# SyncE reads the register values of four expert tiles at once, for all tiles, in a fused attention and mixture-of-experts kernel

## The chip, the cores and the metric

One core of one Trainium2 chip runs the whole program. The metric is device time in microseconds of one execution, given as the median of several. The profile is of one execution; its times count from the span's start.

## What is computed

Attention over four images with keys that are pooled 4 x 4, then a mixture of eight experts in which each row goes to the one expert with the highest score:

```python
kv_pool = kv.reshape(B, H // r, r, W // r, r, C).mean(axis=(2, 4))
k = v = kv_pool.reshape(B, -1, C) @ w_sr
a = softmax(scale * (q @ k.transpose(0, 2, 1)))
x = (a @ v).reshape(B * S, D)                 # 49152 rows of 128
expert_idx = argmax(logits of x against expert_emb, axis=1)
for e in range(E):                            # 8 experts, F = 1024
    mask = expert_idx == e
    h = np.maximum(x[mask] @ w1[e], 0.0)
    out[mask] = gate_w[mask, None] * (h @ w2[e])
```

## The kernel before, in words

**Attention.** 96 steps of 512 query rows (`NSTEP`, `Q`). A step computes scores on TensorE (L810; the first 16 steps L803), takes the maximum on DVE (L821), the exponential on ACT (L840), and splits the result into two fp16 parts, `phi` and `plo`. SyncE issues two DMA transposes for each half of a step, `pthi` and `ptlo` (L904), and TensorE multiplies them with the values (L926). Queries come through a load (L702) and, in most steps, a DMA transpose `qT` (L790). Four steps are a group: its 2048 rows are scored against the experts, and POOL scatters them with indirect DMAs into the table `xs_rows`, each to the region of its expert (L207).

**Experts.** When a group is placed, `select` cuts from what lies in the regions eight tiles (`PER`) of 256 rows, each of one expert. It writes the first row of each tile into eight columns of `off_i` (L1454) and the row of the tile's weights in `w_prep` into eight columns of `wi_i` (L1373), with one instruction each, `wi_i` last. A value of `E * P` or more in `wi_i` means that the weights lie in the buffer already, and the copy is skipped. There are 184 such tiles (`NA`), and after them up to 23 of 128 rows for what is left over, in stages.

SyncE loads a tile. `load_w(t)` (L1563) takes the tile's value of `wi_i` into a register and issues a copy of 1026 KB of weights under a condition (L1568) into one of three buffers `wbuf`. `load(t)` (L1574) takes the value of `off_i`, issues a DMA transpose of 256 rows into `x` (L1592) and a small copy of gates and row numbers `m` (L1593). Both take the register from `value` (L1552), which has two ways: for the tiles up to `NA - PER` = 176 one register is read for one tile, with a check of its bounds (L1554); for the eight tiles after that and the remainder, the first tile of four reads four registers in one instruction without that check (L1557), and `held` keeps them for the other three. TensorE then computes the first layer (L1625), ACT and DVE the ReLU in two fp16 parts `hh` and `hl` (L1632, L1637), TensorE the second layer (L1661), ACT or DVE the gated output (L1681, L1684), and POOL scatters it into the output (L207).

**The order.** No order is left to the hardware: a planner in the program (`Plan.run`) simulates all engines while the kernel is built and writes the instructions in the order that it finds. `pl.add(engine, length, key, ...)` enters an operation with its planned length in us, a due time as key, and what it depends on. The planner takes the engine that is free first, and from its operations that are ready the one with the smallest key. For SyncE it also keeps a time `moved` at which the DMA engines will have moved what is queued, and adds a part for longer issues:

```python
turned = op.dur > 0.5
free[eng] = max(
    free[eng] + (0.55 if turned else 0.0), self.moved - (0.93 if turned else X["ahead"])
)
```

`X["ahead"]` is 2.284. `kw`, the key of a weight copy, is 1 us ahead of that of the tile's `x`, and `x` is due `X["lead"]` = 18.786 us ahead of the tile's first matmul. So a planned length of a SyncE operation sets when the planner holds the following transposes and loads for ready, and through them in which order it writes the work of the other engines.

Of the kernel before, what the change touches and what calls it, by code (L numbers as in the profile page):

```python
# [46 lines left out]
    lead=18.786, x=-14.465, r=0.691, s=-1.205, p=14.572, x0=3.032, r0=2.092, s0=1.377, p0=5.813, qt0=-0.263,  # L47
# [12 lines left out]
def attention_moe(  # L60
# [11 lines left out]
    nc = tc.nc  # L72
# [12 lines left out]
    Q = 512  # L85
# [8 lines left out]
    PER = G * Q // T  # L94
    NSEL = NGRP - LAG
    NA = NSEL * PER
    NTILE = NA + (NT - NA * T) // TR + E - 1
# [5 lines left out]
    OB = 8  # L103
    XB = 6
# [149 lines left out]
    class Plan:  # L254
# [9 lines left out]
        def add(self, eng, dur, key, fn, *deps, dma=None, take=None, free=None, hold=False, lands=False, port=False):  # L264
            op = Op(eng, dur, key, fn, deps, dma, take, free, hold, lands, port, self.stage)
            self.ops.append(op)
            return op
# [1279 lines left out]
    def size(t):  # L1547
        return T if t < NA else TR
# [1 line left out]
    held = {}  # L1550

    def value(name, src, t, top):  # L1552
        if t < NA - PER:
            return nc.sync.value_load(src[0:1, t : t + 1], min_val=0, max_val=top)  # L1554
        i = t // 4 * 4
        if (name, i) not in held:
            held[name, i] = nc.values_load_multi_w_load_instructions(  # L1557
                src[0:1, i : min(i + 4, NTILE)], engines=[nc.sync.engine], min_val=0, max_val=top,
                skip_runtime_bounds_check_because="the rows and weights of a tile are bounded where they are worked out",
            )[1]  # L1560
        return held[name, i][t - i]

    def load_w(t):  # L1563
        if NA <= t < NA + 2:
            wbuf.append(kvs.tile([P, WD], F16, tag="kvt", name=f"wbuf{WB + t - NA}", bufs=2))
        w = value("w", wi_i, t, E * P + 4096)
        row = nc.s_assert_within(w, 0, (E - 1) * P, skip_runtime_bounds_check_because="the copy is skipped then")
        nc.sync.dma_start(out=wbuf[turn_of(t)][:, :WC], in_=wprep[ds(row, P), :], cond=w < E * P)  # L1568

    xr, late = [], []  # L1570
    ML = 18
    XR = 4 * NK // (4 * TR)

    def load(t):  # L1574
        n = size(t)
        o = value("x", off_i, t, NROW - n)
        if t == NA - ML:
            late.append(wk.tile([P, NK], F32, tag="p", name="ml", bufs=NP))
        if t < NA:
            if t < NA - ML:  # L1580
                m = wk2.tile([P, n // P, 2], F32, tag="m", name=f"m{t}", bufs=OB + 2)
            else:
                m = late[0][:, (t - NA + ML) * 8 : (t - NA + ML) * 8 + n // P * 2].rearrange("p (j c) -> p j c", c=2)
            x = wk2.tile([P, 2, n], F16, tag="x", name=f"x_{t}", bufs=XB)
        else:
            i, j = divmod(t - NA, XR)
            if j == 0:
                xr.append(wk.tile([P, NK], F32, tag="p", name=f"xr{i}", bufs=NP).bitcast(F16))
            x = xr[i][:, j * 2 * n : (j + 1) * 2 * n].rearrange("p (h q) -> p h q", h=2)
            m = wk2.tile([P, n // P, 2], F32, tag="mr", name=f"m{t}", bufs=NTILE - NA)  # L1590
        src = xs[ds(o, n), :]
        a = nc.sync.dma_start(out=x, in_=src.bitcast(F16)[:, 0 : 2 * C], transpose=True)  # L1592
        b = nc.sync.dma_start(out=m, in_=src[:, CG : CG + 2].rearrange("(j p) c -> p j c", p=P))  # L1593
        if t < NA:
            for ins in (a, b):
                for key in keys[t // PER + LAG + 1 :]:
                    tc.declare_no_dep(ins.ins, group=key, reason="rows of earlier groups only")
                tc.add_to_no_dep_group("loads", ins.ins)
        ts[t].update(x=x, m=m)

    def turn_of(t):
        return t % WB if t < NA else (WB, WB + 1, *[(NA + i) % WB for i in range(WB)])[(t - NA) % (WB + 2)]
# [4 lines left out]
    def wide(t):  # L1607
        return t >= NA

    def units(t):  # L1610
        return NF * size(t) // 512
# [39 lines left out]
    def l2_lo(t, u):  # L1651
        l2_terms(t, u, ts[t].pop(("hl", u)), (0,))
# [53 lines left out]
    add, chain = pl.add, pl.chain  # L1706
    uses = {}

    def turn(tag, bufs):

        u = uses.setdefault(tag, [])
        return (u[-1][:1] if u else []) + (u[-bufs] if len(u) >= bufs else [])

    def took(tag, op):
        uses[tag].append([op])
        return op

    def reads(tag, *ops):
        uses[tag][-1].extend(ops)
# [121 lines left out]
    stores, v_whole, whole_k, kf_next = [], [], [], []  # L1841
# [295 lines left out]
    for k in range(NSTEP):  # L2137
        if k % SPB == SPB // 2 and k // SPB + 1 < B:
            kv_ops(k // SPB + 1)
        t = step_ops(k)  # L2140
        if k % G == G - 1:
            t = group_ops(k // G, t)
# [12 lines left out]
    def wb_turn(t):  # L2155
        u = uses.setdefault("wb", [])
        before = t - WB if t < NA else t - WB - 2
        return u[-1][:1] + u[before] if before >= 0 and not NA <= t < NA + 2 else []

    for t in range(NTILE):  # L2160
        pl.stage = sum(t >= NA + n for n in STAGES)
        s, n, nu = TM[t], t // PER, units(t)
        w = (X["di"] if KA + t * T // Q < NSTEP else X["db"]) / 8
        whole = t < NA
        deps = [x_open, chosen[n][-1], *placed[n + LAG]] if whole else [x_open, rest[-1], *x_pads, x_dummies, *placed[NGRP - 1]]
        tx, tm = ("mx", "m" if t < NA - ML else "ml") if whole else ("mxr", "mr")
        if t >= NA - ML:
            turn(tx, 1), turn(tm, 1)
        ld = add("SP", 2.5 if t < NA - PER else 1.5 if t % 4 else 2.5, s - (X["lead"] if whole else X["leadr"]), lambda t=t: load(t), *deps, *(turn(tx, XB) if whole else ()), *turn(tm, OB + 2 if t < NA - ML else NTILE), dma=1.3 * size(t) / Q)
        took(tx, ld)  # L2170
        took(tm, ld)
        first = NA <= t < NA + 2
        kw = TM[NA] - X["wr"] + 9.0 * (t - NA) if first else s - X["lead"] - 1.0 if whole else s - X["leadr"] - 8.0
        lw = took("wb", add(
            "SP", 0.5 if t < NA - PER else 0.2 if t % 4 else 1.2, kw, lambda t=t: load_w(t), *deps[:2], *stores, *wb_turn(t),
            dma=3.6 if t < WB or first or NA + 1 < t < NA + 7 else 0.08, hold=first,
        ))
        o1, o2, ol = None if whole else o1, None, None
        f = 512 / size(t)
        for u in range(nu):  # L2180
            key = s + (u + X["m"]) * w
            tag, swap = ("ph2", x_last) if wide(t) and u % 2 else ("ph", x_swap)
            own = None if tag == "ph2" else f"ph{t}_{u}"
            o1 = add(
                "PE", 0.65, key, lambda t=t, u=u: l1(t, u), ld, lw, swap, o1, *(() if own else turn(tag, 2)), take=own
            )
            if not own:
                took(tag, o1)
            k2 = key + X["l2"] * w
            hi = took("hh", add("ACT", 0.48, k2 - X["h"], lambda t=t, u=u: h_hi(t, u), o1, *turn("hh", 4)))  # L2190
            lo = took("hl", add("DVE", 0.6, k2 - X["h"] + 0.3, lambda t=t, u=u: h_lo(t, u), hi, *turn("hl", 6), free=own))
            if not own:
                reads(tag, hi, lo)
            po = "po2" if wide(t) and t % 2 else None
            took_po = None if po else f"po{t}"
            o2 = add(
                "PE", 0.45, k2, lambda t=t, u=u: l2(t, u), hi, o2, *((*turn(po, 1), x_last) if u == 0 and po else ()),
                take=took_po if u == 0 else None,
            )
            if u == 0 and po:  # L2200
                took(po, o2)
            reads("hh", o2, lo)
            ol = add("PE", 0.225, k2 + X["lb"] * w, lambda t=t, u=u: l2_lo(t, u), lo, o2, ol)
            reads("hl", ol)
        reads(tx, o1)
        if gated(t):
            g = add("DVE", 0.08, k2 - X["og"], lambda t=t: o_gate(t), ld, lw, port=True)
            reads("wb", g)
            o = took("o", add("ACT", 1.06 / f, k2 + 0.8, lambda t=t: o_out(t), g, ol, *turn("o", OB), free=took_po))
        else:  # L2210
            o = took("o", add("DVE", 0.66 / f, k2 + 0.8, lambda t=t: o_out(t), ol, *turn("o", OB), free=took_po))
        if po:
            reads(po, o)
        reads("wb", o)
        sc = [
            add("POOL", 1.12, k2 + 4.0 + 1.34 * j, lambda t=t, j=j: o_scatter(t, j), o, dma=0.2) for j in range(size(t) // P)
        ]
        reads("o", *sc)
        reads(tm, o, *sc)
# [38 lines left out]
```

## Time and profile before

| | us |
|---|---|
| median of 3 runs (1941.62 to 1948.85) | 1942.09 |
| the profiled execution's own time | 1946.91 |
| its span, first to last instruction | 1945.2 |
| TensorE matmuls busy in the span | 1906.0 |
| VectorE (DVE) busy | 1675.1 |
| ScalarE (ACT) busy | 1468.7 |
| GpSimd (POOL) busy | 1289.4 |

PE is TensorE's matmul row, PEld its row of weight loads. SP is SyncE; it computes nothing, and all that it does (register reads, waits, DMA issues) is shown in rows that are marked SPq and not counted as busy. A DMA issue's row lasts until SyncE has handed the DMA over; where the instruction waits for a semaphore, that may lie inside the row or ahead of it.

### The profile page before, as it was taken

What the parts mean: (1) busy time and instruction counts of PE and PEld (TensorE: products, weight loads), DVE (VectorE), ACT (ScalarE), POOL (GpSimd) and SP (SyncE); (2) the same over time, 40 slices, a digit from 0 to 9 for tenths busy, and PEclk for the clock granted to TensorE, in tenths of its full rate; (3) what the DMA queues carried; (4) which work ended last, traced back from release to release, by engine and by line L of the source; (5) the groups of instructions that cost most, each with busy time, mean ns of one, the idle gap of its engine ahead of it and who ended that gap; (6) DMA issues with size and microseconds to landing.
All of it is one profiled execution on the core that took longest, in us unless ns stands there. A gap on an engine that the chain in (4) does not pass through costs nothing. (4 is left out here: it accounts for less than half of the span.)

```text
span 1945.2 us, 63642 instructions
## 1 busy us (share of the span) xinstructions
PE 1906.0 (98%) x23536; PEld 1676.3 (86%) x23536; DVE 1675.1 (86%) x4037; ACT 1468.7 (76%) x3162; POOL 1289.4 (66%) x1857
## 2 busy tenths in 40 slices
PE   6999999999999999999999999999999999999998
PEld 5787788888888888888888888888888888889998
DVE  7899999988989879989989988998888888886655
ACT  4887877877787778877778877878878788775553
POOL 2547587678777777676676675756756766666654
PEclk9999999999999999999999999999999999999999
DMA  7998989889988999878989899887878677664353
GB/s 258 250 267 207 205 174 183 165 156 164 170 182 173 190 205 175 172 165 157 193 168 175 180 214 180 171 157 155 176 132 173 149 153 152 148 126 86 107 131 109
DMA packets 870922, 333.23 MB, mean 171 GB/s; under 512 B 825794, under 2 KB 836171, under 8 KB 868432
## 3 DMA queue, kind: packets, MB, share of 16 engines
q1 hardware_dynamic: 844624, 274.95, 71.4%
q0 software_dynamic: 24640, 53.53, 9.7%
q8 instruction: 186, 3.05, 0.7%
q14 instruction: 128, 1.05, 0.2%
q10 hardware_dynamic: 1344, 0.66, 0.1%
HBM read 271.41 MB, written 63.19 MB: 172 GB/s over the span
## 5 line engine op out<-in xcount | busy, mean ns | idle before, releaser
L1632 ACT ACTIVATE hh<-ph 128x512 f16<-128x512 f32 x754 | 447.6, 595 | 224.4 <-PE ph L1625 181.2
L1637 DVE SCALAR_TENSOR_TENSOR hl<-ph,hh 128x512 f16<-128x512 f32 x754 | 513.6, 684 | 109.6 <-ACT hh L1632 103.7
L1625 PE MATMUL ph<-x,wbuf 128*128 128x256 f16 x4416 | 593.2, 273 | 3.2 <-DMA wbuf<-w_prep 2.5
L207 POOL DMA_INDIRECT xs_rows<-rows,pi x384 | 442.0, 1151 | 176.5 <-issue 37.8
L207 POOL DMA_INDIRECT out_dram<-o,m x350 | 382.4, 1093 | 229.0 <-ACT o L1681 45.8
L1625 PEld LDWEIGHTS <-wbuf 128*128 128x128 f16 x4848 | 438.9, 98 | 67.4 <-DMA wbuf<-w_prep 2.9
L1661 PE MATMUL po<-wbuf,hh 128*128 128x128 f16 x6032 | 459.9, 219 | 2.9 <-DVE hl L1637 1.1
L1661 PEld LDWEIGHTS <-hh 128*128 128x128 f16 x6176 | 400.0, 98 | 20.6 <-issue 3.8
L810 PE MATMUL s<-k,qT 128*128 128x512 f16 (+1 forms) x1920 | 364.9, 326 | 1.4 <-DVE nm L821 1.4
L821 DVE CUSTOM_DVE_ANT_0 p<-s,scales,qa 128x768 f32<-128x768 f32 x320 | 323.4, 1011 | 41.6 <-PE s L810 38.9
L875 DVE SCALAR_TENSOR_TENSOR plo<-p,phi 128x768 f16<-128x768 f32 x358 | 350.3, 980 | 5.6 <-ACT phi L861 2.4
L840 ACT ACTIVATE p<-p,nm 128x768 f32<-128x768 f32 x320 | 299.0, 934 | 58.8 <-DVE nm L821 56.8
L926 PE MATMUL xp<-v,pthi 128*128 128x136 f16 (+1 forms) x4392 | 319.7, 223 | 1.4 <-ACT q L738 0.8
L1661 PE MATMUL po<-wbuf,hl 128*128 128x128 f16 x3016 | 291.6, 219 | 0.0
L926 PEld LDWEIGHTS <-pthi 128*128 128x128 f16 x4392 | 278.7, 98 | 14.4 <-issue 2.3
L861 ACT ACTIVATE phi<-p 128x768 f16<-128x768 f32 x310 | 260.9, 844 | 5.9 <-DMA pthi<-phi 2.8
L810 PEld LDWEIGHTS <-qT 128*128 128x128 f16 x1920 | 178.6, 98 | 87.4 <-issue 2.3
L1661 PEld LDWEIGHTS <-hl 128*128 128x128 f16 x3088 | 205.1, 98 | 0.6
L926 PE MATMUL xp<-v,ptlo 128*128 128x136 f16 x2196 | 189.8, 223 | 4.3 <-DMA ptlo<-plo 4.3
L946 ACT ACTIVATE x<-xp,rn 128x135 f32<-128x135 f32 x304 | 96.5, 372 | 76.3 <-DVE rn L938 58.2
L960 POOL TENSOR_TENSOR rows<-x,rows 128x256 f16<-128x256 f32 x192 | 137.2, 719 | 18.2 <-ACT rows L956 13.3
L926 PEld LDWEIGHTS <-ptlo 128*128 128x128 f16 x2196 | 144.0, 98 | 4.8 <-DMA ptlo<-plo 4.8
(416 smaller groups left out, 2043.0 us busy)
## 6 DMA issues: line engine op xcount, KB each, us to landing
wbuf<-w_prep SPq DMA_DIRECT2D x202, 1026.0 KB
q<-in_q_dram SPq DMA_DIRECT2D x48, 512.0 KB
kvt<-in_kv_dram SPq DMA_DIRECT2D x24, 768.0 KB
wf<-in_moe_w_dram SPq DMA_DIRECT2D x16, 512.0 KB
kvt<-in_kv_dram SPq DMA_DIRECT2D x12, 512.0 KB
xs_rows<-rows,pi POOLq DMA_INDIRECT x384
out_dram<-o,m POOLq DMA_INDIRECT x350
w_prep<-wo SPq DMA_DIRECT2D x8, 514.0 KB
```

What stands on the lines that cost most here:

```text
L207: ins = nc.gpsimd.indirect_dma_start(out=dst, out_offset=bass.IndirectOffsetOnAxis(ap=idx, axis=0), in_=src, in_offset=None, bounds_check= ...
L810: nc.tensor.matmul(t[:, lo:hi], qs[:, l, :], r[:, lo:hi], start=i == 0, stop=i == 2)
L821: V.tensor_tensor_reduce(out=p, in0=ks[k].pop(("s", j)), in1=scales[:, 4:5].broadcast_to([P, NK]), scale=ks[k]["fac"], scalar=3.0e38, op0= ...
L840: nc.scalar.activation(out=p, in_=s, func=AF.Exp, bias=ks[k].pop(("nm", j)), scale=1.0 if unscaled(k) else -1.0)
L861: nc.scalar.mul(hi, p, PSC)
L875: V.scalar_tensor_tensor(out=lo, in0=ks[k].pop(("p", j)), scalar=PSC, in1=hi, op0=ALU.mult, op1=ALU.subtract)
L926: nc.tensor.matmul(ks[k]["xp", h][:, i, :e], l[:, c, :], r[:, c, :e], start=n == 0, stop=n == len(terms) - 1, skip_group_check=True,)
L960: nc.gpsimd.tensor_tensor(out=r[:, :, C : 2 * C], in0=ks[k]["x"][:, 2 * h : 2 * h + 2, 0:C], in1=r[:, :, 0:C], op=ALU.subtract)
L1625: nc.tensor.matmul(ph[:, kk * n : (kk + 1) * n], weights(t, o + f, P), r, start=i == 0, stop=i == 2)
L1632: nc.scalar.activation(out=hh, in_=ts[t]["ph", u], func=AF.Relu)
L1637: V.scalar_tensor_tensor(out=hl, in0=ts[t].pop(("ph", u)), scalar=0.0, in1=ts[t]["hh", u], op0=ALU.max, op1=ALU.subtract)
L1661: nc.tensor.matmul(ts[t]["po"][:, j * C : (j + 1) * C], h[:, kk * n + j * P : kk * n + (j + 1) * P], weights(t, f, P), start=u == 0 and i ...
```

## The change

`value` loses its first way: the first tile of each four reads four registers for all tiles. Two planned lengths follow it: the `x` load of a tile becomes 2.5 for the first tile of four and 1.5 for the others (before: 2.5 for all of the first 176), and the weight copy 1.3 and 0.3 (before: 0.5). All other numbers of the plan stay.

```diff
     def value(name, src, t, top):
-        if t < NA - PER:
-            return nc.sync.value_load(src[0:1, t : t + 1], min_val=0, max_val=top)
         i = t // 4 * 4
         if (name, i) not in held:
             held[name, i] = nc.values_load_multi_w_load_instructions(
@@
-        ld = add("SP", 2.5 if t < NA - PER else 1.5 if t % 4 else 2.5, s - (X["lead"] if whole else X["leadr"]), lambda t=t: load(t), *deps, *(turn(tx, XB) if whole else ()), *turn(tm, OB + 2 if t < NA - ML else NTILE), dma=1.3 * size(t) / Q)
+        ld = add("SP", 1.5 if t % 4 else 2.5, s - (X["lead"] if whole else X["leadr"]), lambda t=t: load(t), *deps, *(turn(tx, XB) if whole else ()), *turn(tm, OB + 2 if t < NA - ML else NTILE), dma=1.3 * size(t) / Q)
@@
         lw = took("wb", add(
-            "SP", 0.5 if t < NA - PER else 0.2 if t % 4 else 1.2, kw, lambda t=t: load_w(t), *deps[:2], *stores, *wb_turn(t),
+            "SP", (0.3 if t % 4 else 1.3) if t < NA - PER else 0.2 if t % 4 else 1.2, kw, lambda t=t: load_w(t), *deps[:2], *stores, *wb_turn(t),
```

## Rows read from the trace of the kernel before

**Rows 1.** The page: busy us (share of the span) and instructions of each engine
```profile
PE 1906.0 (98%) x23536; PEld 1676.3 (86%) x23536; DVE 1675.1 (86%) x4037; ACT 1468.7 (76%) x3162; POOL 1289.4 (66%) x1857
```

**Rows 2.** By stretch: length, busy (instructions) of PE, PEld, DVE, ACT, POOL; clock, DMA, GB/s
```profile
0.00:200.00 200.00, 180.32 (x1289) 138.32 (x1290) 175.59 (x437) 149.21 (x298) 100.47 (x124) 0.99 0.95 244
200.00:1850.00 1650.00, 1636.22 (x20834) 1451.67 (x20832) 1447.58 (x3511) 1276.59 (x2788) 1143.02 (x1688) 1.00 0.83 165
1850.00:1945.00 95.00, 89.44 (x1419) 86.33 (x1417) 51.91 (x91) 42.85 (x78) 45.88 (x47) 0.99 0.43 121
```

**Rows 3.** Waits of TensorE's matmuls: us in total, times, longest
```profile
PE xp L926 <- DMA ptlo<-plo: 4.3, 2, 2.3
...
PE ph L1625 <- DMA wbuf<-w_prep: 2.5, 2, 2.1
...
PE xp L926 <- DMA pthi<-phi: 0.6, 2, 0.4
```

**Rows 4.** Register reads on SyncE: ns min/median/max, first and last start
```profile
L1554 SPq FUSED_REGOPS  x352: 147/164/187, 216.2 to 1831.9; - x176
...
L1554 SPq TENSOR_LOAD <-wi_i x176: 263/542/1214, 215.2 to 1831.6; - x176
L1554 SPq TENSOR_LOAD <-off_i x176: 263/288/957, 217.4 to 1813.2; - x176
...
L1557 SPq TENSOR_LOAD <-wi_i x7: 301/304/318, 1830.6 to 1926.4; - x7
```

**Rows 5.** Timeline at 533 us, start and length: SyncE's issues, the matmul that waited
```profile
522.58 1.44 SPq L904 DMA_TRANSPOSE pthi<-phi  x1
525.97 0.09 SPq L1568 DMA_DIRECT2D wbuf<-w_prep  x1
526.17 2.29 SPq L790 DMA_TRANSPOSE qT<-q  x1
528.50 3.88 SPq L904 DMA_TRANSPOSE ptlo<-plo  x1
...
535.35 0.53 PE L926 MATMUL xp<-v,ptlo 128*128 128x136 f16 x6 [2.00 <-DMA ptlo<-plo]
```

**Rows 6.** The same at 706 us
```profile
698.48 5.26 SPq L790 DMA_TRANSPOSE qT<-q  x1
704.76 0.10 SPq L1568 DMA_DIRECT2D wbuf<-w_prep  x1
704.91 1.42 SPq L904 DMA_TRANSPOSE ptlo<-plo  x1
707.54 1.19 SPq L1592 DMA_TRANSPOSE x<-xs_rows  x1
709.00 0.40 SPq L1593 DMA_DIRECT2D m<-xs_rows  x1
...
708.74 0.53 PE L926 MATMUL xp<-v,ptlo 128*128 128x136 f16 x6 [2.29 <-DMA ptlo<-plo]
```

**Rows 7.** Timeline of SyncE's issues in the tail, tiles whose registers are held already
```profile
1846.52 0.43 SPq L1593 DMA_DIRECT2D ml<-xs_rows  x1
1847.08 1.19 SPq L1592 DMA_TRANSPOSE x<-xs_rows  x1
1848.47 0.43 SPq L1593 DMA_DIRECT2D ml<-xs_rows  x1
1849.28 0.08 SPq L1568 DMA_DIRECT2D wbuf<-w_prep  x1
```

**Rows 8.** SyncE's own waits: us in total, times, longest
```profile
SPq L904 <- ACT hh L1632: 74.7, 54, 5.5
```

**Rows 9.** One of attention's two transpose issues on SyncE: ns min/median/max
```profile
L904 SPq DMA_TRANSPOSE ptlo<-plo x183: 1274/1455/5621, 37.9 to 1754.6; - x183
```

**Rows 10.** The page's groups of the experts' first layer: busy us, mean ns, idle before
```profile
L1625 PE MATMUL ph<-x,wbuf 128*128 128x256 f16 x4416 | 593.2, 273 | 3.2 <-DMA wbuf<-w_prep 2.5
...
L1625 PEld LDWEIGHTS <-wbuf 128*128 128x128 f16 x4848 | 438.9, 98 | 67.4 <-DMA wbuf<-w_prep 2.9
```

## The prediction

> **What bounds the kernel now.** I read the page first. TensorE's matmul row is busy 1906.0 of 1945.2 us, and no other engine is above 86% [rows 1]; SyncE computes nothing, so it has no share there. The question is therefore what stands in TensorE's 39 idle microseconds, and which of them SyncE can end. The table by stretches puts them in place [rows 2]: 19.7 in the first 200 us, before an expert tile is loaded, 5.6 in the tail after 1850 us, and 1650.0 - 1636.2 = 13.8 in between, where the changed loads are. The granted clock of that stretch is 1.00, so nothing is lost to the lower level there.
>
> The waits of TensorE name the causes [rows 3]. DMA transfers that SyncE issues end 4.3 (`ptlo`) + 2.5 (`wbuf`) + 0.6 (`pthi`) = 7.4 us of its waits, most of it in three stalls of 2.0 to 2.3 us. `x` is not among the waits at all. The rest of the 13.8 us, 6.4, is for ACT and DVE or too short to be listed. So 7.4 us is what SyncE can give back directly.
>
> **What goes.** Each of the 176 earlier tiles issues two register reads on SyncE, one of `wi_i` (median 542 ns) and one of `off_i` (288 ns), each with a register computation for its bound (164 ns) [rows 4]: 176 x 0.830 + 352 x 0.164 = 146 + 58 = 204 us of SyncE time. A read of four stands in the last tiles already: 304 ns, with no bound behind it [rows 4]. After the change there are 44 + 44 of those, 88 x 0.304 = 27 us. SyncE loses 177 us, 1.0 us per tile; the gaps between the removed instructions come on top. The issue rows show reads and gaps together: an `x` transpose behind a read starts 1.21 us after the issue before it (706.33 to 707.54), without one 0.13 (1846.95 to 1847.08); a `wbuf` copy 1.02 or 1.95 (from 703.74 and 524.02), without one 0.38 [rows 5, 6, 7]. So one read of `off_i` costs between 0.45 (its two medians) and 1.08, one of `wi_i` between 0.64 and 1.57.
>
> No DMA is added, removed or moved to another queue; POOL's stay too. No wait is added: the eight columns of a group are written by one instruction per table, and a tile's load already depends on the last of them, so the three more columns are ready when the first is.
>
> **What of it is on the path.** Little. Tiles follow each other about every 9.2 us (from 215.2 to 1831.6 in 175 steps [rows 4]), so 1.0 us is 11% of SyncE's time; but SyncE often waits itself, longest for the ACT instruction that the order ties its transposes to (74.7 us in 54 waits [rows 8]), and where that is so an earlier SyncE only waits longer. What the shorter `x` loads give is hidden entirely, since TensorE never waits for an `x`; if that cover were gone, a late `x` would cost what a late `ptlo` does, 2.0 to 2.3 us. Stall by stall, with the order of work kept:
> - At 533 us `ptlo` is 2.00 us late. Ahead of its issue stand one `wi_i` read, worth 1.95 - 0.38 = 1.57, and a `qT` transpose; then the issue itself takes 3.88 us [rows 5]. Between 0 and 1.57; I take half, 0.8, since the two issues behind the read are long for reasons that these rows do not show.
> - At 706 us it is 2.29 us late. SyncE stood 5.26 us in a `qT` transpose; the `wi_i` read behind it is worth 1.02 - 0.38 = 0.64 [rows 6].
> - The `wbuf` copy that comes 2.1 us late [rows 3] has its own read directly ahead of it: 0.64 again, the one of the two values that is nearer to the medians (0.542 + 0.164 = 0.71).
>
> Three of four reads vanish, so (0.8 + 0.64 + 0.64) x 3/4 = 1.6 us. Bounds: nothing, and the whole 7.4.
>
> **The planned lengths.** The planner adds 0.55 us to a SyncE operation planned above 0.5. So `x` load and weight copy of a tile go from 3.05 + 0.5 = 3.55 us to (3.05 + 3 x 2.05 + 1.85 + 3 x 0.3) / 4 = 2.99. Measured, the pair takes 1.95 (1846.95 to 1848.90) + 0.46 (to 1849.36) = 2.41 in the tail without reads [rows 7]. With single reads by their medians that is 2.41 + 0.45 + 0.71 = 3.57 at the least, and 3.07 + 1.12 = 4.19 at 706 us [rows 6]; with a read of four each it is 2.41 + 2 x 0.304 / 4 = 2.56. The plan was right or too short by up to 0.6, and becomes too long by 0.4. Since the times at which the plan holds things for ready decide what an engine takes next, the written order on all engines can change. No row of before shows the new order. It could remove all the idle time of the stretch, 13.8, or add as much again. I take nothing: the bounds are equally far, and neither the shorter plan nor the spare 0.4 us says which way.
>
> **Sum.** 1.6 us. The profiled execution took 1946.9 (span 1945.2 and 1.7 around it), 4.8 above the median of the runs, 1942.1. On its own time the sum gives 1945.3, on the median 1940.5: no difference that can be told, since a measurement of this kernel separates about 0.5%, or 9.7 us.
>
> **Rivals.**
> - **A new order with more late transposes (slower).** With shorter loads the planner sees `ptlo` land earlier and puts attention's value matmuls (L926) earlier on TensorE, while the issue of a transpose takes 1.46 us (median) against a planned 0.63 + 0.55 = 1.18 [rows 9]. Each miss costs 2.0 to 2.3 us, as at 533 and 706. The transpose is issued 183 times, two a step, so there are some 91 steps; it decides from five more stalls among them: 5 x 2.15 = 10.8, that is 1952.9, and with eight 1959.3. For: two are there already, and an issue can take 5.6 us. Against: the loads are now planned longer than they take, which gives back 0.4 us per tile. Chance 0.21.
> - **The stalls go (faster).** Earlier issues and the new order together remove more than 9.7 of the 13.8 us; 1928.3 if all goes. It needs waits for ACT and DVE to go too, which SyncE does not set. Chance 0.05.
> - **TensorE has slack that its matmul row hides.** Its weight-load row is busy 1451.7 of the 1650 us [rows 2], 198 idle. But matmuls of the experts' first layer take 593.2 / 4416 = 134 ns each in busy time counted once, against 98 ns of a weight load [rows 10]: (134 - 98) x 4416 = 159 of the 198 us are matmuls that last longer than a load, not slack. Were a tenth of the other 39 us returned, the time would be 1938, no change that can be told. Chance 0.02. The Trainium skill's Perfetto Trace Analysis (Identifying the Most-Contended Engine) says that matmul occupancy is a bad measure of what is left, and the busy share of weight loads a good one; by that rule 14% of the span would be open, an estimate of 270 us from the 86% of the page. The trace does not bear it out where a matmul has 256 moving columns.
> - **The reads do not get cheaper**, because a read of four takes as long as four reads. The tail's 304 ns speak against it [rows 4]. 1942, chance 0.02.
>
> **How the numbers follow.** The forecast has 0.70; with the two last rivals, which end near it, no change has 0.74; faster 0.05, slower 0.21. The range reaches down to 1942.1 - 7.4 = 1934.7, taken as 1934 (the waits for SyncE's transfers gone), and up to 1942.1 + 13.8 = 1956, the idle time of the stretch doubled, which takes in about half of the slower rival. The likeliest case alone spans 1934 to 1951.
>
> **What would show it.** Right: L1557 has 44 + 7 = 51 reads of each table at about 0.3 us and the single reads are gone; `wbuf` and `x` issues stand closer behind their predecessors; TensorE's idle time between 200 and 1850 us stays at 10 to 18 us; SyncE's waits grow by what the reads gave up. Wrong: five or more new stalls of two microseconds in TensorE's waits for `ptlo` or `pthi`, or new and longer ones for ACT and DVE from another order (slower); under 5 us idle in the stretch (faster).

## The result: slower by 0.6%, and the profile after

The changed kernel takes 1956.58 us (median of six runs, 1953.72 to 1960.74), the kernel before 1944.82 in its six runs beside them: a ratio of 1.0061, with a 95% interval of 1.0051 to 1.0072. The forecast was 1940.5 with a range up to 1956.0.

The profiled execution (1956.3 us, span 1954.6) shows where the 9.4 us of its span come from. First the page's busy times and two stretches (columns as in [rows 2]):

```profile
PE 1908.5 (98%) x23536; PEld 1677.5 (86%) x23536; DVE 1679.0 (86%) x4037; ACT 1469.8 (75%) x3162; POOL 1303.2 (67%) x1857
...
200.00:1850.00 1650.00, 1628.85 (x20713) 1443.64 (x20711) 1446.88 (x3503) 1273.71 (x2779) 1152.52 (x1682) 1.00 0.83 165
...
1150.00:1200.00 50.00, 43.18 (x533) 37.83 (x532) 37.17 (x83) 33.75 (x73) 31.60 (x43) 0.93 1.03 198
```

TensorE idles 46.1 us in place of 39.2, and between 200 and 1850 us, where the change acts, 1650.0 - 1628.9 = 21.2 in place of 13.8 [rows 2]. The other 2.5 us are longer busy time. One slice of 50 us holds 6.8 us of the idle time at a granted clock of 0.93; in the kernel before the same slice had 2.6 us and 0.97. What did the reads do? They are as foreseen, 44 + 7 of each table, a little longer than in the tail before [rows 4]:

```profile
L1555 SPq TENSOR_LOAD <-wi_i x51: 297/328/997, 215.6 to 1933.2; - x51
L1555 SPq TENSOR_LOAD <-off_i x51: 293/397/937, 217.4 to 1927.7; - x51
```

TensorE's waits in that stretch of 200 to 1850 us (us in total, times, longest) answer [rows 3]:

```profile
PE po L1659 <- ACT x L946: 6.3, 1, 6.3
PE ph L1623 <- DVE hl L1635: 3.5, 5, 1.1
PE po L1659 <- DVE hl L1635: 2.7, 2, 2.0
PE rk L1100 <- DVE oh L1086: 2.0, 2, 1.4
...
PE xp L926 <- DVE hl L1635: 1.7, 2, 1.2
...
PE v_m L441 <- DVE hl L1635: 1.2, 1, 1.2
```

`ptlo`, `pthi` and `wbuf` are gone from the list: the 7.4 us for SyncE's transfers (7.2 of them in this stretch) were given back. New are one stall of 6.3 us and about 9 us of short waits that the list puts down to DVE's `hl`, which stood at 1.1 + 0.4 us in the same view of the kernel before (the change takes two lines out of the program, so L1637 before is L1635 after):

```profile
PE po L1661 <- DVE hl L1637: 1.1, 1, 1.1
...
PE ph L1625 <- DVE hl L1637: 0.4, 1, 0.4
```

The long stall can be followed in the timelines of the changed kernel, mostly from 1160 to 1178 us: TensorE, ACT, DVE and SyncE, start and length, with the idle time before and its releaser in brackets:

```profile
1166.25 0.61 PE L1659 MATMUL po<-wbuf,hh 128*128 128x128 f16 x8
...
1167.89 0.82 PE L1623 MATMUL ph<-x,wbuf 128*128 128x256 f16 x6
1175.04 1.01 PE L1659 MATMUL po<-wbuf,hh 128*128 128x128 f16 x8 [6.33 <-ACT x L946]
...
1165.36 0.84 ACT L861 ACTIVATE phi<-p 128x768 f16<-128x768 f32 x1
1174.36 0.64 ACT L946 ACTIVATE x<-xp,rn 128x135 f32<-128x135 f32 x2 [8.15 <-DVE rn L938]
...
1164.28 0.68 DVE L1635 SCALAR_TENSOR_TENSOR hl<-ph,hh 128x512 f16<-128x512 f32 x1
1172.88 0.23 DVE L1670 TENSOR_SCALAR m<-m,wbuf 128x2 f32<-128x2 f32 x1 [7.92 <-DMA wbuf<-w_prep]
1173.02 0.95 DVE L875 SCALAR_TENSOR_TENSOR plo<-p,phi 128x768 f16<-128x768 f32 x1
1173.89 0.15 DVE L937 TENSOR_SCALAR rn<-xp 128x2 f32<-128x2 f32 x1
1174.07 0.17 DVE L938 RECIPROCAL rn<-rn 128x2 f32<-128x2 f32 x1
...
1155.94 5.01 SPq L904 DMA_TRANSPOSE ptlo<-plo  x1
1161.13 1.19 SPq L1590 DMA_TRANSPOSE x<-xs_rows  x1
1162.59 0.39 SPq L1591 DMA_DIRECT2D m<-xs_rows  x1
1163.07 1.89 SPq L904 DMA_TRANSPOSE pthi<-phi  x1
1165.35 0.34 SPq L1566 DMA_DIRECT2D wbuf<-w_prep  x1
```

Read it from the bottom. SyncE issues the weight copy of tile 98 at 1165.35; it moves 1026 KB in earnest (most copies are skipped, since the buffer holds the expert's weights already), and DVE sees it landed only at 1172.9. DVE has already come to the small product of that tile's gates with a factor that lies beside the weights (L1670, called the gate product below). It waits 7.92 us for the copy, and attention's `plo` and `rn` are queued behind it; ACT waits 8.15 us for `rn`, and TensorE waits for ACT. Behind the stall the eight matmuls take 1.01 us, where the eight at 1166.25 took 0.61: the granted clock is 0.77 between 1165 and 1180 us, a mixture of its two levels, 2.4 and 1.2 GHz. TensorE was standing idle in this stall when it fell to 1.2 GHz, for 6.8 us.

Not all of this stall is new. In the kernel before, TensorE waited 2.13 us for the same copy of tile 98, the third stall of the prediction, and its clock stood at 1.2 GHz for 3.4 us behind it:

```profile
1163.98 0.72 PE L1625 MATMUL ph<-x,wbuf 128*128 128x256 f16 x5 [2.13 <-DMA wbuf<-w_prep]
...
1157.61 0.35 SPq L1568 DMA_DIRECT2D wbuf<-w_prep  x1
```

So the stall is 4.2 us longer than it was. It could only arise at a few places: between 200 and 1830 us, the trace's DMA packets show copies that move data for nine tiles alone, 0 to 2, 48 to 50 and 96 to 98. DVE's wait for copies at gate products is 12.8 us in this stretch, against 3.9 before (there L1672):

```profile
DVE m L1670 <- DMA wbuf<-w_prep: 12.8, 4, 7.9
DVE m L1670 <- DMA xs_rows<-rows,pi: 2.6, 1, 2.6
```
```profile
DVE m L1672 <- DMA wbuf<-w_prep: 3.9, 3, 2.5
```

A second kind of wait grew with it. ACT writes the first part of a step's queries (L769) into a buffer that an earlier `qT` transpose must have read; DVE writes the second part behind it (L777). ACT's waits there for the transpose rose from 2.0 to 15.7 us, first before, then after:

```profile
ACT q L769 <- DMA qT<-q: 2.0, 2, 1.8
```
```profile
ACT q L769 <- DMA qT<-q: 15.7, 10, 3.8
```

One of TensorE's waits on the list after goes straight back to it: at 733 us it waits 1.2 us behind DVE, which had waited 2.6 us for ACT, and ACT 3.8 us for the transpose.

Part of what SyncE gained goes into waiting: before its `x` transposes it waits 77.4 us for TensorE's `ph`, against 27.7 in the same rows of before.

```profile
SPq L1590 <- PE ph L1623: 77.4, 52, 5.3
```

### The profile page after: what moved, and what is told of

It reads as the page before. It is cut to its first block, busy times and chain, and to the rows that moved or that the text cites. A ratio compares the mean times of both kernels' runs of the same rounds, so it can differ in the third digit from the quotient of the medians.

```text
span 1954.6 us, 62685 instructions
## 1 busy us (share of the span) xinstructions
PE 1908.5 (98%) x23536; PEld 1677.5 (86%) x23536; DVE 1679.0 (86%) x4037; ACT 1469.8 (75%) x3162; POOL 1303.2 (67%) x1857
## 5 line engine op out<-in xcount | busy, mean ns | idle before, releaser
L1635 DVE SCALAR_TENSOR_TENSOR hl<-ph,hh 128x512 f16<-128x512 f32 x754 | 513.4, 683 | 100.2 <-ACT hh L1630 95.3
L207 POOL DMA_INDIRECT out_dram<-o,m x350 | 389.6, 1113 | 214.7 <-ACT o L1679 41.5
L960 POOL TENSOR_TENSOR rows<-x,rows 128x256 f16<-128x256 f32 x192 | 140.4, 736 | 16.2 <-ACT rows L956 10.9
```

What stands on the lines that cost most here:

```text
L207: ins = nc.gpsimd.indirect_dma_start(out=dst, out_offset=bass.IndirectOffsetOnAxis(ap=idx, axis=0), in_=src, in_offset=None, bounds_check= ...
L960: nc.gpsimd.tensor_tensor(out=r[:, :, C : 2 * C], in0=ks[k]["x"][:, 2 * h : 2 * h + 2, 0:C], in1=r[:, :, 0:C], op=ALU.subtract)
L1635: V.scalar_tensor_tensor(out=hl, in0=ts[t].pop(("ph", u)), scalar=0.0, in1=ts[t]["hh", u], op0=ALU.max, op1=ALU.subtract)
```

## The experiments

Sixteen runs in four sets, five rounds each beside the kernel before. In the third set the kernel before took 1945.9 us, in the others 2004.0, 2005.3 and 2003.7; ratios are therefore what is compared, and only the changed kernel (1.0061 and 1.0048) and its tied form (0.9943 and 0.9957) show how far a ratio moves from one set to another. The last two columns are what DVE waited for transfers at gate products, and what ACT waited for `qT` transposes at L769, between 200 and 1850 us in the profiled execution.

| kernel | set | ratio | interval | DVE at gates, us | ACT for `qT`, us |
|---|---|---|---|---|---|
| before | | 1 | | 4.3 | 2.0 |
| changed (first result) | | 1.0061 | 1.0051 to 1.0072 | 15.4 | 15.7 |
| changed_again | 2 | 1.0048 | 1.0031 to 1.0064 | 12.7 | 14.5 |
| reads_alone | 1 | 0.9965 | 0.9946 to 0.9983 | 1.4 | 0 |
| lengths_alone | 1 | 1.0119 | 1.0086 to 1.0152 | 18.0 | 27.6 |
| gate98_tied | 2 | 1.0050 | 1.0033 to 1.0067 | 6.6 | 16.2 |
| x_lengths_only | 2 | 1.0054 | 1.0034 to 1.0075 | 11.5 | 9.6 |
| w_lengths_only | 2 | 1.0021 | 1.0004 to 1.0038 | 5.1 | 0 |
| lengths_near | 3 | 0.9989 | 0.9980 to 0.9998 | 3.7 | 0 |
| gate_tied | 1 | 0.9943 | 0.9923 to 0.9963 | 0 | 11.3 |
| gate_tied_again | 4 | 0.9957 | 0.9939 to 0.9975 | 0 | 16.7 |
| before_gate_tied | 1 | 0.9987 | 0.9965 to 1.0010 | 0 | 1.2 |
| reads_gate_tied | 3 | 0.9939 | 0.9926 to 0.9953 | 0 | 0 |
| reads_near_gate_tied | 4 | 0.9961 | 0.9946 to 0.9977 | 0.3 | 2.8 |
| x_gate_tied | 3 | 1.0010 | 1.0001 to 1.0020 | 0 | 10.7 |
| x_near_gate_tied | 4 | 1.0019 | 1.0000 to 1.0038 | 0 | 10.0 |
| w_gate_tied | 3 | 0.9985 | 0.9976 to 0.9994 | 0 | 0 |
| both_near_gate_tied | 4 | 0.9996 | 0.9975 to 1.0016 | 0 | 11.1 |

### The two halves of the change apart

`reads_alone` is the kernel before without the two lines of single reads:

```diff
-        if t < NA - PER:
-            return nc.sync.value_load(src[0:1, t : t + 1], min_val=0, max_val=top)
```

> The reads of four with the planned lengths of before: every engine's work stands in the order of before, only SyncE's reads differ. Theory A (the loss is the new order that the planned lengths make): no slower than before, ratio 0.995 to 1.001, and TensorE's waits for DMA transfers (7.4 us before) fall below 5. Theory B (a read of four costs something itself, by holding SyncE or by coming too early): the whole loss is here, ratio 1.004 to 1.008.

`lengths_alone` is the changed kernel with those two lines put back.

> The planned lengths of after with single reads: every engine's work stands in the order of after. Theory A (order): as slow as the changed kernel or slower, since SyncE is later too, ratio to before 1.006 to 1.012. Theory B (the reads): as before, ratio 0.998 to 1.002.

Theory A holds, on both sides. The reads alone make the kernel faster by 0.35%, 7 us of 2004 (3.4 to 10.8); the lengths alone make it slower by 1.2%, 24 us. Multiplied they give 1.0084, somewhat above the 1.0048 measured for both together in the next set, within what the two intervals allow (1.0032 to 1.0135). DVE's waits at gate products go with it. Here are the rows of `reads_alone` and of `lengths_alone`:

```profile
DVE m L1670 <- DMA wbuf<-w_prep: 0.8, 1, 0.8
```
```profile
DVE m L1672 <- DMA wbuf<-w_prep: 17.2, 4, 9.4
```

With early reads and the old order, copies are there when DVE comes, but for 0.8 us; with late reads and the new order, it stands at tile 98 for 9.4 us. TensorE's own waits for transfers in `reads_alone` are 1.9 us for a `ptlo` and 1.2 for the `wbuf` of tile 98, 3.1 together, below the 5 that theory A set.

> The changed kernel once more, on the chip of the other runs of this set. Theory A: ratio 1.005 to 1.008, as it was; between the new order with single reads (1.012) and the reads of four in the old order (0.9965) the two effects add, so 1.012 x 0.9965 = 1.008.

Measured 1.0048, just under the 1.005 to 1.008 expected; the first result, 1.0061, lies in that.

### All gate products moved, and one alone

`gate_tied` adds one dependency to the plan: the gate product of a tile may be written on DVE only behind the tile's first matmuls, which read the same weights. It adds no wait on the chip. `before_gate_tied` has the same edit on the kernel before.

```diff
+            of = o1 if u == 0 else of
...
-            g = add("DVE", 0.08, k2 - X["og"], lambda t=t: o_gate(t), ld, lw, port=True)
+            g = add("DVE", 0.08, k2 - X["og"], lambda t=t: o_gate(t), ld, lw, of, port=True)
```

> The changed kernel, but the planner may write a tile's gate product on DVE only behind that tile's first first-layer matmuls, which need the same weight copy. Theory A1 (within the new order it is the one stall of TensorE at 1168 us, 6.3 us, where DVE stood 7.9 us at a gate product for a weight copy, plus the lower clock after it): DVE's waits for the copy fall from 12.8 us to under 4, and the time comes down by 5 to 9 us, to 1947 to 1952. Rival A2 (the loss is many small waits, and any other order has as many): the waits for the copy vanish as well, but the time stays at 1953 to 1960.

> The same tie in the kernel before. A1: it loses little, as DVE waits 3.9 us for weight copies there: 1940 to 1946. A2 (an order other than that of before costs several us, whatever it is): 1948 to 1958.

DVE waits at no gate product any more in either. The changed kernel wins back all that it had lost and more: 0.9943 in the first set, where 1.0048 stood in the second, some 20 us and far beyond the 5 to 9 of A1. The kernel before gains next to nothing, as A1 has it. But the edit gives a new order to all engines, so it does not say that the one stall was the cause. `gate98_tied` can tell: it has the tie for tile 98 alone. In it DVE's instruction stands eight places later, and nothing else differs on any engine.

```diff
+            g = add("DVE", 0.08, k2 - X["og"], lambda t=t: o_gate(t), ld, lw, of if t == 98 else None, port=True)
```

> The changed kernel with one single instruction moved: DVE's gate product of tile 98, which waited 7.9 us for its weight copy, stands eight places later in DVE's order; every other engine's order is untouched. A1 (this stall is most of the loss): the stall at 1168 us and the lower clock behind it go, 6 to 9 us less than the changed kernel, ratio to before 1.001 to 1.004. A2 (the loss is many small waits): 0 to 3 us less, since the tiles after it wait for the same copy anyway.

A1 falls: 1.0050 against 1.0048, where it asked for 6 to 9 us less; no gain at all is still within A2's 0 to 3 us. TensorE's waits between 1150 and 1230 us, of `changed_again` and of `gate98_tied`, say why:

```profile
PE po L1659 <- ACT x L946: 4.7, 1, 4.7
```
```profile
PE ph L1623 <- DMA wbuf<-w_prep: 3.1, 1, 3.1
PE xp L926 <- DVE hl L1635: 1.5, 2, 1.2
```

Once DVE no longer stands in the way, TensorE itself reaches the tile's first matmuls before the copy is there: 3.1 of the 4.7 us come back in a wait for it. The copy was late, and the gate product was only the first to find out. The longer wait in the second row, 1.15 us, has another root. SyncE issues a `qT` transpose two places behind the weight copy; ACT waits for it, DVE for ACT, and the `hl` that the list names stands in DVE's order behind that. Rows of `gate98_tied`:

```profile
1192.12 4.56 SPq L790 DMA_TRANSPOSE qT<-q  x1
...
1199.91 0.72 ACT L769 ACTIVATE q<-q,qa 128x512 f16<-128x512 f32 x1 [7.50 <-DMA qT<-q]
...
1200.67 0.75 DVE L777 SCALAR_TENSOR_TENSOR q<-q,qa,q 128x512 f16<-128x512 f32 x1 [7.62 <-ACT q L769]
...
1202.08 0.87 PE L926 MATMUL xp<-v,pthi 128*128 128x136 f16 x12 [1.15 <-DVE hl L1635]
```

The granted clock of this stretch of 80 us is 0.98 in both runs.

### Which of the lengths

`x_lengths_only` is the changed kernel with the weight copy planned at 0.5 again for the first 176 tiles, `w_lengths_only` with the `x` load at 2.5 again:

```diff
-"SP", (0.3 if t % 4 else 1.3) if t < NA - PER else 0.2 if t % 4 else 1.2, kw
+"SP", 0.5 if t < NA - PER else 0.2 if t % 4 else 1.2, kw
```
```diff
-"SP", 1.5 if t % 4 else 2.5, s
+"SP", 2.5 if t < NA - PER else 1.5 if t % 4 else 2.5, s
```

> Reads of four, the new planned lengths for the x loads alone, the weight copy planned at 0.5 as before. Theory A with the x lengths as the part that matters (2.5 to 1.5 brings the planned landing forward): as the changed kernel, 1.004 to 1.009. Rival A3 (any new order lands somewhere by chance): anywhere from 0.995 to 1.010, decided by whether a gate product stands ahead of a copy that really moves.

> Reads of four, the new planned lengths for the weight copies alone (1.3 and 0.3), x loads planned at 2.5 as before. Theory A with the x lengths as the part that matters: near the reads of four in the old order, 0.995 to 1.000. Rival A3: anywhere from 0.995 to 1.010.

The `x` lengths alone cost as much as the whole change; the weight lengths alone, with 1.0021, lie above the 0.995 to 1.000 of theory A; only A3's wide range holds them. To see what an order change without meaning does, `lengths_near` takes `reads_alone` and plans the `x` load at 2.4:

```diff
-"SP", 2.5 if t < NA - PER else 1.5 if t % 4 else 2.5, s
+"SP", 2.4 if t < NA - PER else 1.5 if t % 4 else 2.5, s
```

> Reads of four, no tie, the x load planned at 2.4 in place of 2.5 and nothing else: a change too small to mean anything, but the order differs from place 1956 of TensorE on. Theory L: anywhere from 0.996 to 1.006, as far from 0.9965 as the other orders. Theory G: it follows DVE's waits for gate products: 0.996 to 0.998 where these stay under 3 us, 1.002 or more where they exceed 8.

It gives 0.9989, 0.24% above `reads_alone` for a tenth of a microsecond in the plan; the two stand in different sets and their intervals just touch. Theory L's range holds it. Theory G had no figure for the 3.7 us that DVE waited at gates; 2.6 of them were for a weight copy, and for less than 3 us it asked for 0.996 to 0.998.

### The same orders with the gates tied

The edit of `gate_tied` once more, on `reads_alone`, `x_lengths_only` and `w_lengths_only`.

> Reads of four, planned lengths of before, gate products tied behind the tile's first first-layer matmuls. Theory G (what separates the orders is how long DVE stands at gate products for copies that really move; with all gates tied every order is alike): 0.993 to 0.996, as the tied changed kernel (0.9943). Theory L (each order falls where it falls, and the tie only drew another one): anywhere from 0.993 to 1.006.

> The same tie with the new lengths for the x loads alone (untied: 1.0054). Theory G: 0.993 to 0.997. Theory L: anywhere from 0.993 to 1.006; if x lengths themselves are bad, 1.002 or more.

> The same tie with the new lengths for the weight copies alone (untied: 1.0021). Theory G: 0.993 to 0.997. Theory L: anywhere from 0.993 to 1.006.

The tie lowers each: 0.9965 to 0.9939 (the intervals overlap), 1.0054 to 1.0010, 1.0021 to 0.9985, each compared across two sets. But the orders do not meet, as theory G wants; 0.7% lies between the first two. TensorE's waits from 200 to 1850 us show what is left, first `reads_gate_tied` in full, then the top of `x_gate_tied`:

```profile
PE xp L926 <- DMA ptlo<-plo: 1.6, 1, 1.6
PE s L810 <- DVE nm L821: 1.4, 1, 1.4
PE v_m L441 <- DVE m L685: 1.4, 1, 1.4
PE po L1659 <- ACT o L1679: 0.5, 1, 0.5
PE rk L1100 <- DVE oh L1086: 0.2, 1, 0.2
PE po L1659 <- ACT hh L1630: 0.2, 1, 0.2
```
```profile
PE xp L926 <- DVE hl L1635: 4.5, 3, 2.5
PE po L1659 <- DVE hl L1635: 2.8, 4, 1.0
PE ph L1623 <- DVE hl L1635: 2.5, 1, 2.5
```

In the order with shorter `x` loads, 9.8 us are waits for DVE's `hl`, of which the other has none on its list. No gate product is behind them, but followed back in the timelines the three longest have two roots. At 715.7 and 1174.0 us (2.5 and 1.6 us) DVE had waited 4.8 and 4.4 us for ACT's L769, and ACT 5.4 and 4.3 us for a `qT` transpose; at 418.3 us (2.5 us) DVE had waited 4.4 us for POOL in `select`. The totals of `x_gate_tied` between 200 and 1850 us; `reads_gate_tied` has neither row:

```profile
ACT q L769 <- DMA qT<-q: 10.7, 4, 5.4
```
```profile
DVE q L777 <- ACT q L769: 9.2, 2, 4.8
```

Four more runs asked whether the loss belongs to the `x` lengths; three of them plan the `x` loads of the first 176 tiles 0.1 us shorter than a tied kernel above (2.4 and 1.4 in place of 2.5 and 1.5, or 2.4 in place of 2.5), the fourth is `gate_tied` again.

> The changed kernel with the tied gate products, beside its neighbours. If its ratio of 0.9943 belongs to the kernel and not to the chip of that set, it is 0.992 to 0.997 again.

> Tied, weight copy planned at 0.5, x loads at 2.4 and 1.4: the neighbour of the kernel that gave 1.0010. X lengths matter: 0.999 to 1.003. Each order by itself: as likely 0.994 to 0.998 as above.

> Tied, weight copy planned at 1.3 and 0.3, x loads at 2.4 and 1.4: the neighbour of the tied changed kernel. Neighbours alike: 0.992 to 0.997. Each order by itself: 0.993 to 1.002.

> Tied, weight copy planned at 0.5, all x loads at 2.4: the neighbour of the kernel that gave 0.9939, and the tied form of the one that gave 0.9989. Neighbours alike: 0.992 to 0.996. Each order by itself: 0.993 to 1.002. If the tie helps every order, it is below 0.9989 either way.

The tied changed kernel keeps its ratio (0.9957). Neighbours lie 0.0022, 0.0009 and 0.0039 apart, the tied kernels 0.0071. That an order close in lengths is close in time is therefore not shown: the last pair, in one set, lies more than half of that spread apart, and "neighbours alike" missed its range there (0.9996 for 0.992 to 0.997; 0.9961 for `reads_near_gate_tied` is just above its 0.996). The new `x` lengths without the new weight lengths stay above 1.000 both times. That isn't the `x` lengths by themselves, since with the weight lengths beside them the same `x` lengths give 0.9957 and 0.9996.

One feature of the orders does follow the `x` lengths. In all ten profiles of kernels with the new `x` lengths (1.5 or 1.4 for three tiles of four), ACT waits 9.6 to 27.6 us for `qT` transposes; in the eight others it waits 0 to 2.8. It doesn't set the time alone, since the tied changed kernel has 11.3 and 16.7 us and is among the fastest. What else decides between these orders stays open, and no run changed the `qT` transposes by themselves.

In all six orders that ran with and without the tie, the one with it has the lower ratio, by 0.13% to about 1%; in the kernel before and in `reads_alone` this is within the uncertainty. Since each tie also draws a new order, theory L's share in it isn't separated.

**The best version.** `reads_gate_tied`, reads of four with the planned lengths of before and the gates tied, takes 1934.29 us beside 1945.87: 0.9939. It beats both kernels; from `gate_tied` (0.9943 and 0.9957, other sets) it can't be told.

## Why the prediction was wrong

- **What goes: right.** 51 reads of each table, at 328 and 397 ns where 304 was taken; 32 us of SyncE time for the 88 new ones and not 27, of the 204 that went.
- **What of it is on the path: right in sign, mis-sized.** The sum had 1.6 us with bounds of 0 and 7.4. `reads_alone` gives 0.35%, 7.0 us, and its interval (3.4 to 10.8) leaves out 1.6. The working counted three stalls and moved each by the read directly ahead of it. Since the order is that of before, the same three matmuls can be looked up in `reads_alone`: the wait of 2.00 us at 533 us is gone, where the working allowed at most 1.57, that of 2.29 at 706 is 1.86, that of 2.13 for the copy is 1.22. That is 3.4 us for a term of 1.6, so what a SyncE that is 1 us per tile ahead does beyond the one read was left out. Where the rest came from can't be shown, since no profile of the kernel before was taken in that set, where it took 3% longer.
- **The planned lengths: the step that failed.** "I take nothing: the bounds are equally far, and neither the shorter plan nor the spare 0.4 us says which way." No row of before showed the new order, and a term that could go either way by 13.8 us was put at nothing. The lengths cost 1.2% with single reads (24 us of 2004), some 0.8 to 1.0% with the reads of four. Lengths nearer to the measured ones did not give a better order: of the five untied orders with reads of four, the old lengths' has the lowest ratio.
- **The slower rival: right in its side, wrong in the transfers and the engine that it named.** It named late `ptlo` transposes, five or more of 2 us. Not one is on the list after. What came late for its place in the new order were other transfers: a weight copy that the plan takes for skipped (0.08 us) and that moves 1026 KB (12.8 us of DVE's waits at gate products, 3.9 before), and `qT` transposes (15.7 us of ACT's waits, 2.0 before). They held DVE and ACT, and only through them TensorE. The rival gave a reason, that a planner with shorter loads sees transposes land earlier; for `qT` it fits, but it was not tried. Moving the one gate product brought nothing back, so these waits show where the loss appears, and which of them costs how much stays open. The prediction's list of signs had "new and longer ones for ACT and DVE from another order", and that is what came; its sum took nothing for it, and its chance of 0.21 came from the wrong place.
- **The clock: left out.** The prediction read a granted clock of 1.00 as nothing lost. That is a rounded mean: behind the 2.13 us stall of before lie 3.4 us at 1.2 GHz, and 6.8 us within and behind the longer one after. A stall was priced at its wait alone.
- **The range.** Its upper end was the stretch's idle time doubled, 1942.1 + 13.8. The idle time of the stretch rose by 7.4, and busy time and clock cost more. The median of six runs of before is 2.7 above the three that the range stood on; on that footing the end would have been 1958.6 and held, with the direction still wrong. Nor was the change too small to tell: the measurement separated some 0.1%, not 0.5%.
- **TensorE's hidden slack: not seen.** The best order has a weight-load share of 87% with 30.8 us of idle matmul row (span 1932.8, busy 1902.0), so its time went down with the idle row, as the rejection of this rival had it.

## What to carry to other kernels

Where a planner writes the order of an in-order machine, changing a cost in it is two changes, the instruction and the order; run each without the other before believing either, as the one here is worth -0.35% and the other +1.2%. An instruction that is ready early and needed late (here a product of 0.1 us) is better not written ahead of its need on a busy engine, when what it waits for is a transfer whose length depends on the data: the tie lowered the ratio in six orders of six, clearly in four. When a stall is traced to one instruction, move that one alone: here most of the wait went on to the next reader of the same late copy. And follow a wait back past the engine that is named first: here `hl` was more than once only the last in a chain that began at a `qT` transpose.

## What the runs showed of the hardware that was not expected

The same kernel before took 1946 us in the third set and 2004 to 2005 in the other three, 3% apart, with granted clocks (means of whole executions) of 0.996 to 0.999 there and 0.990 to 0.999 in the others. The second and the third set ran on the same chip, so it isn't the chip alone. In the first, second and fourth set TensorE has idle time that ends with no releaser in the profile, shown as "issue". Of the changed kernel, the list of the first result (1956.6 us) has no such rows; that of `changed_again` (2014.1 us) has, among all waits of TensorE, these:

```profile
PE po L1659 <- issue: 11.4, 21, 1.1
PE xp L926 <- issue: 7.8, 17, 1.0
PE ph L1623 <- issue: 2.3, 8, 0.5
```

They are 21.5 of the 59 us that lie between the two spans (2013.2 and 1954.6), and another 21.5 are longer busy time of TensorE's matmuls (1930.0 and 1908.5); the cause was not tried. A register read on SyncE, finally, took 293 ns at the least for four values and 263 for one, so four at once cost about as much as one.
